# One ring for all first-layer weights, and preparation loads on GpSimd's queue

## The chip, the cores and the metric

The kernel runs on one core of a Trainium2 chip. Its time is the device time of the whole program in microseconds (us). Before the change three runs took 1879.51, 1882.88 and 1885.13 us, a median of 1882.88. TensorE (PE) does the matmuls, VectorE (DVE), ScalarE (ACT) and GpSimd (POOL) the work on elements. SyncE (SP), ACT and POOL also issue DMAs, each from a queue that it serves in order.

## The reference

```python
attn = softmax(q @ mean_pool8(k).T / 8) @ mean_pool8(v)     # 8 batches, 8 heads, 576 tokens, 64 wide
x    = attn as [4608, 512]
h    = x @ w_in                                             # [4608, 2048]
x2   = (s * relu(h)**2 + b) @ w_out                         # [4608, 512]
out  = (sigmoid(x2 @ w_gate) * (x2 @ w_val)) @ w_out2       # 1536 wide inside
```

Activations are float32. The weights of both layers come as 64-bit words and are turned into float32 on the chip. Every product of the two layers is made of three matmuls on a high and a low part of each operand.

## The kernel before, in words

The first layer works on blocks of 512 tokens: block 0 plainly, then four pairs of blocks by a scheme with fewer products (seven instead of eight; `LEFT`, L286), whose operands are sums and differences of the four quarters of the weights and of the activations. The second layer does the same with its weights. Attention runs beside the first layer in 18 units of 256 tokens, two units for each block, some time ahead of it.

A list of slots orders the first layer (L794). Slots 0 to 15 are block 0, then each pair `p` has 40 slots: slot 16 + 40 p + x with chunk x = 8 z + m, z the group of products and m one of eight row blocks. A slot makes up to one `h` step (`emit_h`, L259: 12 matmuls L269 to L271 with the tile `wi`, 512 KB) and one chunk of products (`mm_chunk`, L357: 6 or 12 matmuls L370 to L372 with the tile `wr`). In block 0 the products are `emit_x` (L419 to L421). From slot 16 on the order of PE and SP is the program's own (L835); the order of DVE, ACT and POOL is made by a planner that simulates the program.

**Weights.** For block 0, `load_wi` and `load_wo` load 64-bit words into a `raw` buffer (three of them, `rawp`), `split_wi` and `split_wo` convert them (`convert`, L78: one ACT and three DVE operations) and split them into a high and a low part (ACT, then POOL, L56 and L57). The results stay as tiles for PE and are stored to DRAM as `w1d` and `s1d` (list `later`, emptied by `store_later` at the start of the next slot, on SP up to slot 19 and on POOL after). All later blocks load these back on SP: `load_wi` (L137) three steps ahead into three buffers `wi`, `fetch_s` (L307, L312) into three buffers `wr`, each as soon as the buffer is free.

**Preparation.** In slots 16 to 31 `prep_s` makes the sums of quarters of the second weight, eight turns of two slots. Part 0 loads four tiles `s1d` into two `raw` buffers (L186, SP). Part 1 adds on DVE (L191), works on POOL (L179: four operations and the running sum `wsum`), splits (ACT, DVE) and hands four stores to POOL. `prep_bias` (L205) then sums `wsum` with the constant `b` on PE (`bps`, L212), at the start of slot 32, behind its `h` step. The bias is used by `put_x` (L344), which ends a group of products; for the first pair that is first at slot 33. From slot 33 on `prep_w2` (L228) prepares one second-layer block in eight slots (nine parts, 12 blocks; two parts a slot from x = 13 of the last pair): three loads of 512 KB into `raw` (L72, SP) and nine stores from POOL to `w7d` and `wo2d`. From step NS - 13 `gen_x` (L754) makes the first operands of the second layer.

Of the kernel before, what the change touches and what calls it, by code (L numbers as in the profile page):

```python
# [9 lines left out]
F32R = mybir.dt.float32r  # L10
I32 = mybir.dt.int32
# [8 lines left out]
def pooled_attention_two_ffn(ctx, tc, q, k, v, v_left, w_in, w_out, s_in, b_in, w_gate, w_val, w_out2, out):  # L20
# [46 lines left out]
    wo2d = [dram.tile([128, 2, 512], F32, name=f"wo2d{m}") for m in range(M2)]  # L67
    x2d = [dram.tile([128, KD, n], F32, name=f"x2d{j}") for j, (_, n) in enumerate(blocks)]

    def load64(src):  # L70
        raw = rawp.tile([128, 1024], I32, tag="raw", name="raw")
        nc.sync.dma_start(out=raw, in_=src.bitcast(I32))  # L72
        return raw

    def cv_tile():
# [21 lines left out]

    w1_stack = ExitStack()
    xp = w1_stack.enter_context(tc.tile_pool(name="xp", bufs=2))
    wi_p = w1_stack.enter_context(tc.tile_pool(name="wi_p", bufs=3))  # L100
    rawp = w1_stack.enter_context(tc.tile_pool(name="rawp", bufs=3))
    us_p = w1_stack.enter_context(tc.tile_pool(name="us_p", bufs=1))
    gs_p = w1_stack.enter_context(tc.tile_pool(name="gs_p", bufs=17))
    wr_p = w1_stack.enter_context(tc.tile_pool(name="wr_p", bufs=3))
    at_stack = ExitStack()
    at1 = at_stack.enter_context(tc.tile_pool(name="at1", bufs=1, side="right"))
    at2 = at_stack.enter_context(tc.tile_pool(name="at2", bufs=2, side="right"))
# [14 lines left out]
    bias = const.tile([128, KD], F32, name="bias")  # L122

    def wi_tile(i):
        t = wi_p.tile([128, 2, KD, 128], F32R, tag="wi", name="wi")
        wi[i] = t[:, 0], t[:, 1]
        return t.rearrange("p two k f -> p two (k f)")

# [45 lines left out]
    def prep_s(m, part):  # L174

        h0, h1 = slice(0, 256), slice(256, 512)

        def tt(o, x, y, op):
            nc.gpsimd.tensor_tensor(out=o, in0=x, in1=y, op=op)  # L179

        if part == 0:
            prep["s"] = []
            for xs in ((0, 7), (1, 3)):
                t = raw_tile().bitcast(F32).rearrange("p (two f) -> p two f", two=2)
                for h, x in zip((h0, h1), xs):
                    nc.sync.dma_start(out=t[:, :, h], in_=s1d[x][m])  # L186
                prep["s"].append(t)
        else:
            a, c = (t[:, 1] for t in prep["s"])
            for t in prep["s"]:  # L190
                nc.vector.tensor_tensor(out=t[:, 1], in0=t[:, 0], in1=t[:, 1], op=ALU.add)  # L191
            tt(c[:, h1], a[:, h1], c[:, h1], ALU.add)
            tt(a[:, h1], a[:, h0], a[:, h1], ALU.subtract)
            tt(a[:, h0], c[:, h1], a[:, h0], ALU.subtract)
            tt(c[:, h0], c[:, h0], a[:, h0], ALU.subtract)
            if m == 0:
                nc.gpsimd.tensor_copy(out=wsum, in_=c)
# [30 lines left out]
    def prep_w2(m, part):  # L228
        h0, h1 = slice(0, 256), slice(256, 512)
        if part == 0:  # L230
            prep["g"] = load64(w_gate[m])
        elif part == 1:
            prep["v"] = load64(w_val[m])
        elif part == 2:
            raw = prep["g"]
            prep["gt"] = convert(raw, cv_tile())
            store_split(w7d[m][:, :, 256:768], raw, prep["gt"])
        elif part == 3:
            prep["vt"] = convert(prep["v"], cv_tile())
            store_split(w7d[m][:, :, 0:256], raw_tile(), prep["vt"][:, h0])  # L240
        elif part == 4:
            gt, vt, c = prep["gt"], prep["vt"], cv_tile().bitcast(F32)
            for o, a, b_, op in ((c[:, h1], gt[:, h0], vt[:, h0], ALU.subtract), (vt[:, h0], vt[:, h0], vt[:, h1], ALU.add),
                                 (c[:, h0], vt[:, h0], gt[:, h0], ALU.subtract), (gt[:, h1], gt[:, h1], c[:, h0], ALU.subtract)):
                nc.gpsimd.tensor_tensor(out=o, in0=a, in1=b_, op=op)
            prep["c"] = c
        elif part == 5:
            store_split(w7d[m][:, :, 768:1280], prep["v"], prep["vt"])
        elif part == 6:
            store_split(w7d[m][:, :, 1280:1792], raw_tile(), prep["c"])  # L250
        elif part == 7:
            store_split(w7d[m][:, :, 1792:2048], raw_tile(), prep["gt"][:, h1])
            prep["o"] = load64(w_out2[m])
        else:
            store_split(wo2d[m], prep["o"], convert(prep["o"], cv_tile()))

# [95 lines left out]
    def keep(p, name, pair):  # L352
        acc[p, name] = [us_p.tile([128, 512], F32, tag=f"u{name}{d}", name="us") for d in range(2)]
        for o, a in zip(acc[p, name], pair):
            nc.scalar.activation(out=o, in_=a, func=ACTF.Copy)

    def mm_chunk(p, c):  # L357
        j, (z, m) = 1 + 2 * p, divmod(c, H1)
        if m == 0:
# [15 lines left out]
        if z == 0:  # L375
            keep(p, "p", acc[p, 0])
        elif z == 1:
            for d, a in enumerate(acc.pop((p, 0))):
                put_x(j, d, a)
        elif z == 2:  # L380
            keep(p, "v", acc[p, 2])
        elif z == 3:
            u, v = acc[p, "p"], acc[p, "v"]
            c12 = [cvp.tile([128, 512], F32, tag="cv", name="c12") for _ in range(2)]
            for d in range(2):
                add(u[d], acc[p, 3][d], u[d])
            for d in range(2):
                add(c12[d], acc[p, 2][d], u[d])
            for d in range(2):
                add(v[d], v[d], u[d])  # L390
                put_x(j + 1, d, c12[d])
            del acc[p, 3], acc[p, 2]
        else:
            u, v = acc.pop((p, "p")), acc.pop((p, "v"))
            for d in range(2):
                add(v[d], acc[p, 5][d], v[d])
                add(u[d], acc[p, 5][d], u[d])
            for d in range(2):
# [283 lines left out]
    def turns(u, t):  # L682
        turn(u, t, 0)
        turn(u, t, 1)

    with tc.manual_schedule():
        load_kv(0, "k")
        load_q(0, 2)
# [10 lines left out]
        nc.vector.tensor_tensor(out=mask[:, 2:3], in0=mask[:, 0:1], in1=mask[:, 1:2], op=ALU.subtract)  # L699
        pool_k(0, 0, nc.vector)  # L700
        pool_k(0, 1, nc.vector)
        load_wi(0)
# [4 lines left out]
        load_wi(1)  # L707
        probs(0, 0)
        probs(0, 1)
        norm(0, 0, True)  # L710
# [9 lines left out]
        place_left(0)  # L720
        turns(0, 1)
        norm(1, 0, True)
        split_wi(0)
# [6 lines left out]
        split_wi(1)  # L730
        turns(1, 1)
    if True:
        values(1, 0)
        values(1, 1)
        load_wi(2)
        load_q(2)
        load_q(3)
        NS = len(steps)
        LAG = 2


        pairs = [(1024 * p, 512) for p in range(NB // 2)]
# [46 lines left out]
            sub(b21, b21, b22)  # L789
            put(3, b21)  # L790

        chunks = [(None, i) for i in range(M1)] + [(p, x) for p in range(NB1) for x in range(5 * H1)]  # L794
        NSLOT = len(chunks)
        hidden, used, made, done = {}, [], {}, {}
        for slot, (p, x) in enumerate(chunks):
            if p is None:
                hidden[slot] = x
                ready, turn_ = slot + 5, slot + 6  # L800
            else:
                if x < 4 * H1:
                    hidden[slot if p == 0 or x > 1 else slot - H1] = M1 * (1 + 2 * p) + x
                ready, turn_ = slot, slot + LAG
                if p == 0 and x < H1:
                    ready, turn_ = M1 + 5 + x // 2, M1 + 6 + x // 2
            made.setdefault(ready, []).append((p, x))
            done.setdefault(turn_, []).append((p, x))
            if p is None or x >= 3 * H1 or x % 2:
                used.append((turn_, p, x))  # L810
        asked = M1

        def mm(slot):
            for p, x in done.get(slot, []):
                if p is None:
# [15 lines left out]
        for slot, (p, x) in enumerate(chunks):  # L831
            i = hidden.get(slot)
            swap = p is not None and x == 4 * H1 + 1
            if slot == M1:
                pe_order.enter_context(tc.manual_schedule(engines={mybir.EngineType.PE, mybir.EngineType.SP}))  # L835
            store_later(slot < M1 + 4)
            for fn, args in events.pop(2 * slot, []):
                fn(*args)
            if i is not None:
                load_wi(i + 3)  # L840
                if not swap:
                    emit_h(i)
            for m, r in parts.get(slot, []):
                prep_w2(m, r)
            if M1 <= slot < 2 * M1:
                prep_s(*divmod(slot - M1, 2))
            if slot == 2 * M1:
                prep_bias()
            if slot < M1:
                split_wi(i + 2)  # L850
            if 4 <= slot < M1 + 4:
                split_wo(slot - 4)
            if 2 <= slot < M1 + 2:
                load_wo(slot - 2)
            late = []
            for p1, x1 in made.get(slot, []):
                if p1 is None:
# [12 lines left out]
                    prep_chunk(p1, x1, 1)  # L870
            if swap and i is not None:
                emit_h(i)
            while asked < len(used) and used[asked - 3][0] <= slot:
                _, p1, x1 = used[asked]
                fetch_s(p1, x1 - (x1 < 3 * H1))
                asked += 1
            if p is not None and 4 * H1 - 2 <= x < 5 * H1 - 2:
                reload(p, x - 4 * H1 + 2)
            if i == NS - M1:
# [185 lines left out]
```

## Time and profile before

| | |
|---|---|
| median of three runs | 1882.88 us |
| profiled execution | 1877.16 us, span 1875.3 us |
| PE busy | 1732.0 us (92%), mean granted clock 0.964 |
| DVE, ACT, POOL busy | 1073.2, 751.1, 473.6 us |
| DMA | 464.94 MB, mean 248 GB/s |

The first layer ends at about 1050 us; from there PE is never idle for long until the end. "Idle before" and "waits" name the time in which an engine had nothing running and what it waited for; an engine named SPq, POOLq or ACTq is its DMA queue. A wait of several causes is put down to the one that came last. PEclk is the clock that TensorE was granted, as a part of 2.4 GHz. A row of a timeline gives start and duration in us.

### The profile page before, as it was taken

The page shows a single profiled execution, that of the slowest core. Times are in us where ns is not written, and L with a number is a line of the kernel's source. Part 1 is how long each engine was busy: PE and PEld are TensorE (multiplying, and loading weights), DVE is VectorE, ACT ScalarE, POOL GpSimd, SP SyncE. Part 2 cuts the span into 40 slices and gives each one's busy share as a digit, 9 for nine tenths or more (in the row PEclk, how much of TensorE's full clock was granted, in tenths as well). Part 3 has the DMA queues.
Part 4 walks back from the last instruction along what each step waited for, and adds up shares of the span by engine and source line. Part 5 has one row for each costly group of instructions (what it writes and reads, how often), then busy time and mean ns, then how long its engine had stood idle before and what let it go on. Part 6 is the DMA issues. An engine that isn't in the chain of part 4 may idle for free.

```text
span 1875.3 us, 22252 instructions
## 1 busy us (share of the span) xinstructions
PE 1732.0 (92%) x7880; PEld 1428.1 (76%) x7880; DVE 1073.2 (57%) x1653; ACT 751.1 (40%) x1331; POOL 473.6 (25%) x558
## 2 busy tenths in 40 slices
PE   5899776998999899999849999999999999999999
PEld 4677665876888688877737788888888888888887
DVE  7788554776775868576546544454545544544211
ACT  3676443645664456456534322222222222222111
POOL 4644655435730655005430000100010001000100
PEclk7899987999999999999979999999999999999999
DMA  6878987887976888677856755665576558555675
GB/s 240 284 240 287 337 284 251 279 312 250 372 271 223 288 311 308 226 274 264 320 203 208 251 187 200 252 225 202 201 252 225 184 184 292 185 190 211 224 239 181
DMA packets 153917, 464.94 MB, mean 248 GB/s; under 512 B 16336, under 2 KB 34256, under 8 KB 153808
## 3 DMA queue, kind: packets, MB, share of 16 engines
q1 hardware_dynamic: 127344, 388.55, 59.1%
q0 software_dynamic: 16672, 57.16, 8.5%
q10 hardware_dynamic: 9792, 17.83, 2.5%
q8 instruction: 63, 1.03, 0.2%
q14 instruction: 46, 0.38, 0.1%
HBM read 379.59 MB, written 83.89 MB: 247 GB/s over the span
## 4 chain that ended last, share of the span: by engine, by line
PE 71%; DMA 12%; DVE 11%; POOL 2%; ACT 2%; issue 2%; SPq 1%; ACTq 0%; POOLq 0%; DVEq 0%
PE acc L967 5%; PE pc L912 5%; PE acc L969 5%; PE acc L968 5%; PE pc L913 5%; PE pc L911 5%; PE hps L269 4%; PE hps L271 4%; PE hps L270 4%; PE pb L911 4%; PE pb L912 4%; PE pb L913 4%; DMA raw<-in 4%; PE acc L370 3%; PE acc L371 3%; PE acc L372 3%
## 5 line engine op out<-in xcount | busy, mean ns | idle before, releaser
L269 PE MATMUL hps<-xl,wi 128*128 128x512 f32 (+1 forms) x584 | 237.9, 407 | 51.8 <-DMA wi<-w1d 44.8
L917 DVE TENSOR_TENSOR wk<-pc,wk 128x512 f32<-128x512 f32 x192 | 132.4, 690 | 240.4 <-PE pc L913 240.4
L271 PE MATMUL hps<-xh,wi 128*128 128x512 f32 (+1 forms) x584 | 232.3, 398 | 1.1 <-POOL wi L57 1.1
L270 PE MATMUL hps<-xh,wi 128*128 128x512 f32 (+1 forms) x584 | 232.1, 397 | 0.0
L370 PE MATMUL acc<-gl,wr 128*128 128x512 f32 x448 | 183.0, 409 | 17.7 <-DMA wr<-s1d 10.4
L977 POOL DMA_DIRECT2D out<-eo x32 | 17.4, 544 | 705.1 <-ACT eo L975 702.3
L371 PE MATMUL acc<-gh,wr 128*128 128x512 f32 x448 | 177.9, 397 | 0.0
L372 PE MATMUL acc<-gh,wr 128*128 128x512 f32 x448 | 177.5, 396 | 0.0
L928 ACT ACTIVATE g<-pb 128x512 f32<-128x512 f32 x60 | 35.9, 599 | 346.7 <-PE pb L913 346.7
L269 PEld LDWEIGHTS hps<-xl,wi 128*128 128x128 f32 x584 | 114.2, 196 | 78.4 <-issue 38.5
L57 DVE TENSOR_TENSOR gl<-gs,gh 128x512 fp32r<-128x512 f32 x176 | 149.5, 862 | 37.1 <-ACT gh L56 34.3
L911 PE MATMUL pc<-xo,w 128*128 128x512 f32 x432 | 168.1, 389 | 0.0
L912 PE MATMUL pc<-xo,w 128*128 128x512 f32 x432 | 168.1, 389 | 0.0
L913 PE MATMUL pc<-xo,w 128*128 128x512 f32 x432 | 168.0, 389 | 0.0
L57 POOL TENSOR_TENSOR raw<-cv,raw 128x512 fp32r<-128x512 f32 (+1 forms) x72 | 89.8, 1253 | 295.9 <-ACT raw L56 149.5
L56 ACT ACTIVATE gh<-gs 128x512 fp32r<-128x512 f32 x176 | 107.3, 627 | 114.0 <-DVE gs L296 98.7
L56 ACT ACTIVATE gh<-g 128x512 fp32r<-128x512 f32 x124 | 77.8, 628 | 154.2 <-DVE g L929 141.7
L911 PE MATMUL pb<-xo,w 128*128 128x512 f32 x336 | 131.4, 391 | 2.2 <-DMA w<-w7d 2.2
L271 PEld LDWEIGHTS hps<-xh,wi 128*128 128x128 f32 x584 | 113.6, 195 | 25.8 <-POOL wi L57 1.6
L57 DVE TENSOR_TENSOR gl<-g,gh 128x512 fp32r<-128x512 f32 x124 | 106.5, 859 | 44.7 <-ACT gh L56 40.1
L912 PE MATMUL pb<-xo,w 128*128 128x512 f32 x336 | 131.4, 391 | 0.0
L913 PE MATMUL pb<-xo,w 128*128 128x512 f32 x336 | 131.3, 391 | 0.0
(142 smaller groups left out, 3739.5 us busy)
## 6 DMA issues: line engine op xcount, KB each, us to landing
w<-w7d SPq DMA_DIRECT2D x48, 1792.0 KB, 7.7
wi<-w1d SPq DMA_DIRECT2D x128, 512.0 KB, 5.1
wr<-s1d SPq DMA_DIRECT2D x224, 256.0 KB, 4.9
wo<-wo2d SPq DMA_DIRECT2D x108, 512.0 KB, 7.9
raw<-in SPq DMA_DIRECT2D x68, 512.0 KB, 5.8
w7d<-raw POOLq DMA_DIRECT2D x36, 512.0 KB, 5.5
w<-w7d SPq DMA_DIRECT2D x12, 1280.0 KB, 6.8
kv<-in SPq DMA_DIRECT2D x24, 512.0 KB, 6.5
```

The lines of the kernel that those rows point to most:

```text
L56: nc.scalar.activation(out=hi, in_=src, func=ACTF.Copy)
L57: eng.tensor_tensor(out=lo, in0=src, in1=hi.bitcast(F32), op=ALU.subtract)
L269: nc.tensor.matmul(out=ps[:, f], lhsT=hi[:, kk], rhs=c[:, kk, f], start=kk == 0, stop=False)
L270: nc.tensor.matmul(out=ps[:, f], lhsT=hi[:, kk], rhs=a[:, kk, f], start=False, stop=False)
L271: nc.tensor.matmul(out=ps[:, f], lhsT=lo[:, kk], rhs=a[:, kk, f], start=False, stop=kk == KD - 1)
L370: nc.tensor.matmul(out=a, lhsT=w[:, 0, f], rhs=gl, start=begin, stop=False, skip_group_check=True)
L371: nc.tensor.matmul(out=a, lhsT=w[:, 0, f], rhs=gh, start=False, stop=False, skip_group_check=True)
L372: nc.tensor.matmul(out=a, lhsT=w[:, 1, f], rhs=gh, start=False, stop=end, skip_group_check=True)
L911: nc.tensor.matmul(out=ps, lhsT=w[:, 0, x, kk], rhs=r[:, 1, kk, :n], start=first and kk == 0, stop=False, skip_group_check=True)
L912: nc.tensor.matmul(out=ps, lhsT=w[:, 0, x, kk], rhs=r[:, 0, kk, :n], start=False, stop=False, skip_group_check=True)
L913: nc.tensor.matmul(out=ps, lhsT=w[:, 1, x, kk], rhs=r[:, 0, kk, :n], start=False, stop=kk == 1, skip_group_check=True)
L917: nc.vector.tensor_tensor(out=o, in0=ps, in1=b_, op=ALU.add)
```

## The change

- The pool `wi_p` (three buffers) is gone and `wr_p` has six (`RING`). `wi_tile` takes its tile from it, so `wi` and `wr` tiles share one ring.
- Before the slots a list `used` is made: every first-layer weight tile of the ring with the slot in which PE uses it and the slot after which it is free, sorted by use. `ask(slot)`, at the end of a slot, asks for tiles in this order while the tile six places back is free by this slot and the use is at most three slots off. For block 0 asking means `split_wi` or `split_wo`, and the next 64-bit load (`ask_raw`, in the order of use) goes out behind it. The separate calls of `load_wi`, `split_wi`, `split_wo`, `load_wo` and `fetch_s` in the loop are gone.
- The loads of `prep_s` (32 of 256 KB) and of `prep_w2` (36 of 512 KB) are issued from GpSimd (`nc.gpsimd`) instead of SP.
- `store_later` puts stores on SP in slots below 12 instead of below 20.
- `prep_bias` moves from slot 32 to slot 38, and the first pair's first two `put_x` (`put_c11`) from the end of chunk x = 15 to the same place.

```diff
-    def load64(src):
+    def load64(src, eng=None):
         raw = rawp.tile([128, 1024], I32, tag="raw", name="raw")
-        nc.sync.dma_start(out=raw, in_=src.bitcast(I32))
+        (eng or nc.sync).dma_start(out=raw, in_=src.bitcast(I32))
...
-    wi_p = w1_stack.enter_context(tc.tile_pool(name="wi_p", bufs=3))
...
-    wr_p = w1_stack.enter_context(tc.tile_pool(name="wr_p", bufs=3))
+    RING = 6
+    wr_p = w1_stack.enter_context(tc.tile_pool(name="wr_p", bufs=RING))
...
-        t = wi_p.tile([128, 2, KD, 128], F32R, tag="wi", name="wi")
+        t = wr_tile().rearrange("p (two k f) -> p two k f", two=2, k=KD)
...
-                    nc.sync.dma_start(out=t[:, :, h], in_=s1d[x][m])
+                    nc.gpsimd.dma_start(out=t[:, :, h], in_=s1d[x][m])
...
-            prep["g"] = load64(w_gate[m])
+            prep["g"] = load64(w_gate[m], nc.gpsimd)
-            prep["v"] = load64(w_val[m])
+            prep["v"] = load64(w_val[m], nc.gpsimd)
...
-            prep["o"] = load64(w_out2[m])
+            prep["o"] = load64(w_out2[m], nc.gpsimd)
...
+    def put_c11(p):
+        for d, a in enumerate(acc.pop((p, 0))):
+            put_x(1 + 2 * p, d, a)
...
         elif z == 1:
-            for d, a in enumerate(acc.pop((p, 0))):
-                put_x(j, d, a)
+            if p:
+                put_c11(p)
...
-            if p is None or x >= 3 * H1 or x % 2:
-                used.append((turn_, p, x))
+        if p is None or x >= 3 * H1:
+            used.append((turn_, 1, turn_, p, x))
+        elif x % 2 == 0:
+            used.append((turn_, 1, turn_ + (p > 0 or x >= H1), p, x))
+    used += [(slot, 0, slot, "h", i) for slot, i in hidden.items()]
+    used.sort(key=lambda u: u[:2])
...
+    def ask(slot):
+        nonlocal asked
+        while asked < len(used) and (asked < RING or used[asked - RING][2] <= slot) and used[asked][0] <= slot + 3:
+            _, _, _, k, x = used[asked]
+            asked += 1
+            if k == "h" and x < M1:
+                split_wi(x)
+                ask_raw()
+            elif k == "h":
+                load_wi(x)
+            elif k is None:
+                split_wo(x)
+                ask_raw()
+            else:
+                fetch_s(k, x)
...
-            store_later(slot < M1 + 4)
+            store_later(slot < M1 - 4)
...
-                load_wi(i + 3)
...
-            if slot == 2 * M1:
+            if slot == 2 * M1 + 6:
                 prep_bias()
+                put_c11(0)
-            if slot < M1:
-                split_wi(i + 2)
-            if 4 <= slot < M1 + 4:
-                split_wo(slot - 4)
-            if 2 <= slot < M1 + 2:
-                load_wo(slot - 2)
...
-            while asked < len(used) and used[asked - 3][0] <= slot:
-                _, p1, x1 = used[asked]
-                fetch_s(p1, x1 - (x1 < 3 * H1))
-                asked += 1
+            ask(slot)
```

## Rows read from the trace of the kernel before

**Rows 1.** Busy time by stretch: stretch, length, engines' busy us (instructions), PEclk, DMA share, GB/s

```profile
160.00:336.00 176.00, 139.79 (x661) 115.42 (x660) 99.69 (x159) 76.46 (x141) 102.87 (x120) 0.89 0.84 288
200.00:337.00 137.00, 100.79 (x464) 82.24 (x463) 73.38 (x120) 56.06 (x103) 80.66 (x98) 0.86 0.83 283
917.00:985.00 68.00, 35.04 (x137) 27.30 (x136) 34.18 (x45) 29.63 (x53) 28.95 (x37) 0.78 0.64 226
```

**Rows 2.** Waits of PE, 200 to 345 us: line, releaser, us in total, times, longest

```profile
PE bps L212 <- DVE wsum L207: 13.5, 1, 13.5
PE hps L269 <- DMA wi<-w1d: 12.5, 4, 5.9
PE acc L370 <- DMA wr<-s1d: 7.1, 2, 6.8
```

**Rows 3.** Waits of PE, 900 to 1053 us

```profile
PE hps L269 <- DMA wi<-w1d: 32.3, 3, 25.8
```

**Rows 4.** Waits of SP's DMA queue, 150 to 310 us

```profile
SPq L186 <- DMA s1d<-raw: 54.1, 6, 11.3
```

**Rows 5.** Timeline of SP's DMA queue: start, us, line, issue

```profile
211.92 12.20 SPq L186 DMA_DIRECT2D raw<-s1d  x4
...
225.34 0.84 SPq L307 DMA_DIRECT2D wr<-s1d  x2
```

**Rows 6.** Waits of SP's DMA queue, 900 to 985 us

```profile
SPq L72 <- DMA w7d<-raw: 49.1, 4, 32.2
```

**Rows 7.** Timeline of SP's DMA queue in the second stretch

```profile
974.87 0.40 SPq L137 DMA_DIRECT2D wi<-w1d  x1
```

**Rows 8.** Timeline of PE: start, us, line, matmul, shape, count, idle before and its releaser

```profile
286.66 0.63 PE L270 MATMUL hps<-xh,wi 128*128 128x512 f32 x1
287.08 0.63 PE L271 MATMUL hps<-xh,wi 128*128 128x512 f32 x1
...
302.54 2.05 PE L212 MATMUL bps<-cv,wsum 128*128 128x128 f32 x8 [13.54 <-DVE wsum L207]
...
336.26 0.39 PE L271 MATMUL hps<-xh,wi 128*128 128x512 f32 x1
336.50 0.60 PE L607 MATMUL tm<-ident,pm 128*128 128x128 f32 x4
```

**Rows 9.** Timeline of POOL, first and last two turns of prep_s, and one later row

```profile
174.09 3.92 POOL L179 TENSOR_TENSOR raw<-raw 128x256 f32<-128x256 f32 x4 [4.96 <-DVE raw L191]
...
282.65 3.15 POOL L179 TENSOR_TENSOR raw<-raw 128x256 f32<-128x256 f32 x4 [2.64 <-DVE raw L191]
...
287.61 2.82 POOL L152 DMA_DIRECT2D s1d<-raw  x4
296.36 3.13 POOL L179 TENSOR_TENSOR raw<-raw 128x256 f32<-128x256 f32 x4 [5.93 <-DVE raw L191]
299.57 1.77 POOL L179 TENSOR_TENSOR wsum<-wsum,raw 128x512 f32<-128x512 f32 x1
...
927.11 2.19 POOL L57 TENSOR_TENSOR raw<-cv,raw 128x512 fp32r<-128x512 f32 x2
```

**Rows 10.** Groups by line, POOL, 150 to 310 us: busy us, mean ns, idle before

```profile
L152 POOL DMA_DIRECT2D s1d<-raw x28 | 19.8, 806 | 1.9 <-DVE raw L57 1.9
```

**Rows 11.** DMA issues, 160 to 336 us: count, KB each, us to landing

```profile
raw<-s1d SPq DMA_DIRECT2D x32, 256.0 KB, 4.7
s1d<-raw POOLq DMA_DIRECT2D x28, 256.0 KB, 3.3
```

**Rows 12.** Timeline of DVE, 924 to 932 us

```profile
924.55 5.30 DVE L57 TENSOR_TENSOR gl<-gs,gh 128x512 fp32r<-128x512 f32 x1 [0.70 <-ACT gh L56]
...
931.16 0.69 DVE L57 TENSOR_TENSOR gl<-gs,gh 128x512 fp32r<-128x512 f32 x1 [0.70 <-ACT gh L56]
```

**Rows 13.** Part 2 of the page: GB/s in 40 slices of the span

```profile
GB/s 240 284 240 287 337 284 251 279 312 250 372 271 223 288 311 308 226 274 264 320 203 208 251 187 200 252 225 202 201 252 225 184 184 292 185 190 211 224 239 181
```

**Rows 14.** Waits of PE, 0 to 1000 us

```profile
PE tm L607 <- POOL pm L582: 10.5, 6, 3.9
```

More of the change, by code (lines that the diff above doesn't have):

```diff
@@ L684, in turns, with ask_raw, ask_one @@
         turn(u, t, 1)
+    NS = len(steps)
+    LAG = 2
+    chunks = [(None, i) for i in range(M1)] + [(p, x) for p in range(NB1) for x in range(5 * H1)]
+    NSLOT = len(chunks)
+    hidden, used, made, done = {}, [], {}, {}
+    for slot, (p, x) in enumerate(chunks):
+        if p is None:
+            hidden[slot] = x
+            ready, turn_ = slot + 5, slot + 6
+        else:
+            if x < 4 * H1:
+                hidden[slot if p == 0 or x > 1 else slot - H1] = M1 * (1 + 2 * p) + x
+            ready, turn_ = slot, slot + LAG
+            if p == 0 and x < H1:
+                ready, turn_ = M1 + 5 + x // 2, M1 + 6 + x // 2
+        made.setdefault(ready, []).append((p, x))
+        done.setdefault(turn_, []).append((p, x))
+        if p is None or x >= 3 * H1:
[4 more added lines that the diff above has]
+    used.sort(key=lambda u: u[:2])
+    halves = [(k, x) for _, _, _, k, x in used if k is None or k == "h" and x < M1]
+    asked = raws_asked = 0
+    def ask_raw():
+        nonlocal raws_asked
+        if raws_asked < len(halves):
+            k, x = halves[raws_asked]
+            raws_asked += 1
+            if k == "h":
+                load_wi(x)
+            else:
+                load_wo(x)
+    def ask_one():
+        nonlocal asked
+        split_wi(used[asked][4])
+        asked += 1
+    def ask(slot):
+        nonlocal asked
+        while asked < len(used) and (asked < RING or used[asked - RING][2] <= slot) and used[asked][0] <= slot + 3:
+            _, _, _, k, x = used[asked]
+            asked += 1
+            if k == "h" and x < M1:
+                split_wi(x)
+                ask_raw()
+            elif k == "h":
+                load_wi(x)
+            elif k is None:
+                split_wo(x)
+                ask_raw()
+            else:
+                fetch_s(k, x)
     with tc.manual_schedule():
@@ L701, in pooled_attention_two_ffn @@
         pool_k(0, 1, nc.vector)
-        load_wi(0)
+        ask_raw()
         load_kv(0, "l")
@@ L706, in pooled_attention_two_ffn @@
         nc.sync.dma_start(out=b_sb, in_=b_in.unsqueeze(0).to_broadcast([128, 1]))
-        load_wi(1)
+        ask_raw()
         probs(0, 0)
@@ L722, in pooled_attention_two_ffn @@
         norm(1, 0, True)
-        split_wi(0)
+        ask_one()
         values(0, 0)
@@ L729, in pooled_attention_two_ffn @@
         left(1, 1)
-        split_wi(1)
+        ask_one()
         turns(1, 1)
@@ L734, in pooled_attention_two_ffn @@
         values(1, 1)
[L735 removed]
+        ask_raw()
         load_q(2)
         load_q(3)
[L738 to L739 removed]
         pairs = [(1024 * p, 512) for p in range(NB // 2)]
@@ L790, in gen_x @@
             put(3, b21)
[L794 to L808, printed above, removed]
-            if p is None or x >= 3 * H1 or x % 2:
-                used.append((turn_, p, x))
-        asked = M1
         def mm(slot):
@@ L835, in pooled_attention_two_ffn @@
                 pe_order.enter_context(tc.manual_schedule(engines={mybir.EngineType.PE, mybir.EngineType.SP}))
-            store_later(slot < M1 + 4)
+            store_later(slot < M1 - 4)
             for fn, args in events.pop(2 * slot, []):
                 fn(*args)
-            if i is not None:
-                load_wi(i + 3)
-                if not swap:
-                    emit_h(i)
+            if i is not None and not swap:
+                emit_h(i)
             for m, r in parts.get(slot, []):
```

## The prediction, made before the changed kernel ran

> **What bounds the kernel now.** I read three views in this order: the busy time by stretch, the waits of PE, and the issue queue of SP at the places where PE waits. PE is the bound wherever nothing stops it, so I looked for the stretches in which it stops. There are two. From 200 to 337 us PE is busy 100.8 of 137 us at a mean granted clock of 0.86, and from 917 to 985 us it is busy 35.0 of 68 at 0.78 [rows 1].
>
> Stretch A is slots 22 to 38. PE's waits there are 13.5 us for the sum `wsum` in front of the bias product, 12.5 us for the tile `wi`, and 7.1 us for the tile `wr` [rows 2]: 33.1 us. Stretch B lies in the last pair of first-layer blocks (slots 152 to 160): 32.3 us, all for `wi`, 25.8 of them at once [rows 3].
>
> In neither stretch is the transfer slow; it is issued late. SP's queue is served in order, and in A the loads of `prep_s` (L186) stand in it for 54.1 us, waiting until an earlier store has left the `raw` buffer they want [rows 4]. One of them holds the queue from 211.92 for 12.2 us [rows 5], and the `wr` load that PE then waits for stands behind it. In B it is the second-layer preparation load (L72), which waits 49.1 us for `w7d` stores [rows 6]; the load of `wi` goes out right after it, at 974.87 [rows 7].
>
> A stop costs a second time. After a long one the granted clock has dropped from the 2.4 to the 1.2 GHz level, and matmuls start 0.42 us apart instead of 0.24 [rows 8]. About a dozen run so before the clock is back, 12 x 0.19 = 2.3 us. A has four such stops (the 13.5 us, one of 6.8, one of 5.9 and one a little shorter), so 9.2 us; B has two, so 4.6.
>
> **The change part by part.** *SP's queue freed in A.* The 32 loads of `prep_s` leave SP, and its weight loads now wait only for a ring tile. Six tiles in order of use reach three slots ahead, as the two pools of three did, so I give the ring itself nothing: the landing it must cover is the same, and the price if that cover went is one landing a slot. What goes at most is 33.1 + 9.2 = 42.3 us.
>
> *What is late next in A.* The bias product still needs all eight turns of `prep_s`. It is now asked for at slot 38. Before, PE went from its end (302.54 + 2.05) to the same place in slot 38 (336.50) in 31.9 us [rows 8]. With every stall of A but the bias wait gone, PE would have been at slot 32's product at 289.0 - 19.6 (the two DMA waits) - 6.9 (three restarts) = 262.5, and so at slot 38 at 294. Is `wsum` there by then?
>
> The chain of `prep_s` is serial through three `raw` buffers: store, load into the same buffer, add, four GpSimd operations and a sum, split, store. Its first turn began on POOL at 174.09, the last two at 282.65 and 296.36 [rows 9]. So the fastest turn takes 13.7 us, the mean 122.3 / 7 = 17.5. On POOL a DMA issue costs 0.81 us [rows 10]. Four loads are added a turn; those into the free buffer are hidden in the landing of the stores (3.3 us), the other two are not [rows 11]: 2 x 0.81 = 1.6 us, and with a little for a later landing I add 1.9 us a turn (what SP's own issues took there I don't subtract). At 15.6 us a turn the last one starts at 283 and `wsum` is ready 5 us later, at 288; at 19.4 us, at 310 and 315. These are the two ends. A second count decides between them: POOL is busy 80.7 us of A [rows 1], 24 loads of the six turns in it add 24 x 0.81 = 19, together 100 us; with no idle at all that is 300, and with one microsecond lost a turn 306. I take 306. The bias product (2.05 us) then ends at 308 instead of work at that place starting at 336.5: 28.5 us, less 2.3 for the clock after a wait of 13 us: **26 us in A**. The ends give 42 (ready before PE) and 17.
>
> Moving `put_c11` to slot 38 holds two accumulators of PSUM six slots longer. Slots 34 to 41 use the other two, so it costs nothing unless the product slips past slot 42.
>
> *SP's queue freed in B.* At most 32.3 + 4.6 = 36.9 us. The preparation loads now wait on POOL, where nothing of PE's stands behind them so late: no attention is left after slot 150. What can be late next is DVE: it is busy 34.2 us in this stretch [rows 1], about as long as the PE work in it, because conversions of second-layer weights run there at two parts a slot and the first second-stage operands are generated. DVE and ACT work in order, so an operand of PE's can stand behind a conversion whose load has not landed. The ends are all of the 36.9 and less than half (14, if the chain of `raw` buffers still sets the pace through DVE). I take a quarter lost: **27 us in B**.
>
> *Other moves.* The 36 second-layer loads add 36 x 0.81 = 29 us to POOL over 700 us and take as much waiting off SP: nothing, since POOL has idle time beside them outside A; if that cover went it would be the 29 us. Some 16 stores move from SP to POOL in slots 12 to 19, 13 us of POOL before A begins, and the splits of the first block are asked for one slot earlier, on engines that the planner orders. I see nothing that excludes a loss or a gain there: between -6 and +6 us, half the 13 either way; I take 0.
>
> *Sum.* 26 + 27 = 53 us. The profiled execution took 1877.16 us around a span of 1875.3; less 53 that is 1824. The median of the runs, 1882.88, lies 5.7 above the profiled execution, so I predict **1830 us**.
>
> *A rule against it.* One DVE subtraction that elsewhere takes 0.69 us took 5.30 at 924.55 [rows 12], while POOL ran one operation after another; two of them are the 2.19 us at 927.11 [rows 9]. So the two engines do hold each other off here, and more work on POOL makes such runs longer. The Trainium skill, page "SBUF — State Buffer", section "SBUF: two separate sides", says that DVE and GpSimd share one pair of ports under an exclusive lock for a whole instruction, and that descriptors of a DMA issued from GpSimd cannot be written while DVE holds it; the traces agree on the lock, and of starved descriptors they show nothing, since POOL's stores land in 3.3 us and SP's loads in 4.7. By that rule the time would be the first rival's below, by these rows the forecast's.
>
> **The rivals.** *POOL and DVE hold each other off.* If every load on POOL also waits out one DVE operation of 0.69 us [rows 12], a turn takes 19.4 + 4 x 0.69 = 22.2 us, the last one starts at 329, `wsum` comes at 334 and A gives nothing; with 25 us of B the time is 1858. For it: POOL would be nearly full in A. Against: the store landings just named. Chance 0.17. The lock that the Trainium skill states on its page "SBUF — State Buffer" is this rival's ground too.
>
> *Nothing is late next.* If the turns run at 15.6 us and DVE's order keeps conversions behind operands, 42 + 37 = 79 us go: 1804. For it: the last turns already ran at 13.7. Against: POOL has 100 us of work for 94 us. The transfers also speak against it: A and the slots before it move 288 GB/s over 176 us [rows 1], 50.7 MB; by 294 instead of 336 that would be 378 GB/s, above the best slice of the page, 372 [rows 13]. For the forecast's 306 it is 347. Chance 0.15.
>
> *It goes slower.* The wait is not removed, it moves to POOL's queue, and behind it there stand the probabilities `pm`, on which PE's transposes wait already (10.5 us in six places) [rows 14]. If the planner puts a waiting load in front of most of them, SP's 54.1 and 49.1 us of waiting reach PE again by that way, and the 68 issues of 0.81 us, 55 us, come on top of them on the same queue. With a third of these 55 on PE's path the time is 1882.9 + 18 = about 1900; it decides once more than 53 us of waits at `pm` and at the operands are new. Against: POOL is idle 56 of A's 137 us, and POOL's order is the planner's, not written out. Chance 0.08.
>
> *It does not do what it says.* SP may stop again, now at loads of `wr` that read what `prep_s` stored late (third group of products, slots 34 to 41), with `wi` behind them. If all of A's gain goes so and B's is eaten by conversions, the time stays within 0.3%. Chance 0.06.
>
> **How the numbers follow.** The forecast has 0.54, with its own range of 1812 to 1848 (17 to 42 in A and 14 to 37 in B, not both ends at once). Faster by over 0.3% are the forecast, the first rival and the second: 0.54 + 0.17 + 0.15 = 0.86. Within 0.3%, about 6 us and all that can be told from no change here: 0.06. Slower: 0.08. For 8 in 10 I leave out the slower end with no change (0.14) and some of the second rival's far side: 1802 to 1863.
>
> **What would show it.** In the trace after, SP's list of waits should hold no L186 and no L72, and POOL's should hold loads of `raw`. PE's wait for `wi` should fall from 44.8 us over the first stage to a few. The bias product should start near 306, with a wait of up to 13 us for `wsum`; a start before 295 is the second rival, after 325 the first. In B the 25.8 us stop should be gone, with small waits for `gl` in its place. New waits at `pm` of over 4 us each would show the slower case. The forecast is wrong if the turns of `prep_s` come further apart than 20 us, or if B still has a stop of over 10 us.

## The result, and the profile after

The changed kernel takes 1854.86 us (median of four runs, 1852.52 to 1861.10) against 1881.2 us before: a ratio of 0.9863, 95% interval 0.9831 to 0.9894. That is 26 us, half of the 53 forecast; it lies in the range of 1802 to 1863, but outside the forecast's own 1812 to 1848. The profiled execution has a span of 1851.4 us against 1875.3.

Where the 23.9 us come from is seen by setting the same matmul of both timelines side by side. Each mark is the start of the first L370 matmul (L374 after) of that slot:

| mark | before | after | after is ahead by |
|---|---|---|---|
| slot 34, third group of the first pair | 315.96 | 276.43 | 39.5 |
| slot 42, behind the bias product of both | 356.15 | 372.88 | -16.7 |
| slot 154 | 916.88 | 922.13 | -5.2 |
| slot 162 | 988.52 | 955.57 | 33.0 |
| first matmul of the second layer | 1053.10 | 1030.82 | 22.3 |
| end of the span | 1875.3 | 1851.4 | 23.9 |

So the first stretch was won and then lost with interest, and the second was won in full. Two smaller pieces moved beside them: 11.5 us won between slots 42 and 154, which the prediction had at nothing, and 10.7 lost at the end of the first layer. These marks come from one execution of each kernel, so a difference of a few us in them is not proof by itself.

The windows of after, with the columns of [rows 1]:

```profile
200.00:337.00 137.00, 96.28 (x500) 80.69 (x498) 79.63 (x124) 57.71 (x104) 83.94 (x103) 0.88 0.70 239
917.00:985.00 68.00, 67.51 (x298) 55.59 (x297) 51.84 (x68) 42.93 (x77) 31.85 (x39) 1.00 0.93 311
```

In the second stretch PE now runs through at full clock where it was busy 35 of 68 us [rows 1]. In the first it does 500 matmuls instead of 464, and yet it stands still at the end of it. PE's waits from 160 to 1050 us say where (line, releaser, us in total, times, longest); SP's longest of 150 to 345 us and POOL's two longest of 160 to 352 us name the two other places:

```profile
PE bps L212 <- POOL cv L245: 50.8, 1, 50.8
PE acc L374 <- DVE c L350: 10.0, 4, 5.0
```

```profile
SPq L307 <- DMA s1d<-raw: 67.8, 6, 17.7
```

```profile
POOL raw L186 <- DMA s1d<-raw: 14.5, 5, 4.8
POOL s1d L152 <- DVE raw L57: 13.8, 7, 4.0
```

No wait for a `wi` tile from DRAM is left where there were 44.8 us [rows 2, 3]. All of the first stretch's loss is one wait, in front of the bias product. The releaser in its row is not to be believed: the product does not read what L245 writes. What it needed last is found in the order of ACT, below.

### The profile page after: what moved, and what is told of

Same layout as the page of the kernel before. It is cut to its first block, busy times and chain, and to the rows that moved or that the text cites. A ratio compares the mean times of both kernels' runs of the same rounds, so it can differ in the third digit from the quotient of the medians.

```text
span 1851.4 us, 22232 instructions
## 1 busy us (share of the span) xinstructions
PE 1717.3 (93%) x7880; PEld 1420.4 (77%) x7880; DVE 1081.0 (58%) x1653; ACT 751.2 (41%) x1331; POOL 536.0 (29%) x646
## 3 DMA queue, kind: packets, MB, share of 16 engines
q0 software_dynamic: 26144, 90.19, 13.7%
q8 instruction: 63, 1.03, 0.2%
## 4 chain that ended last, share of the span: by engine, by line
PE 59%; DMA 8%; DVE 7%; POOL 3%; issue 2%; ACT 1%; SPq 0%; ACTq 0%; DVEq 0%; POOLq 0%
PE pc L945 5%; PE pc L943 5%; PE pc L944 5%; PE acc L999 5%; PE acc L1001 5%; PE acc L1000 5%; PE pb L945 4%; PE pb L943 4%; PE pb L944 4%; PE hps L269 2%; PE hps L271 2%; PE hps L270 2%; PE acc L374 2%; PE acc L375 2%; PE acc L376 2%; DVE gl L57 2%
## 5 line engine op out<-in xcount | busy, mean ns | idle before, releaser
L269 PE MATMUL hps<-xl,wr 128*128 128x512 f32 (+1 forms) x584 | 233.0, 399 | 6.1 <-DVE xl L57 3.9
L271 PE MATMUL hps<-xh,wr 128*128 128x512 f32 (+1 forms) x584 | 229.4, 393 | 0.9 <-POOL wr L57 0.9
L270 PE MATMUL hps<-xh,wr 128*128 128x512 f32 (+1 forms) x584 | 229.2, 393 | 0.0
L374 PE MATMUL acc<-gl,wr 128*128 128x512 f32 x448 | 181.3, 405 | 18.6 <-DVE c L350 10.0
L269 PEld LDWEIGHTS hps<-xl,wr 128*128 128x128 f32 x584 | 112.1, 192 | 28.2 <-DVE xl L57 4.1
L271 PEld LDWEIGHTS hps<-xh,wr 128*128 128x128 f32 x584 | 111.9, 192 | 24.8 <-POOL wr L57 1.2
L270 PEld LDWEIGHTS hps<-xh,wr 128*128 128x128 f32 x584 | 112.1, 192 | 21.4
```

Source lines behind the costliest of these rows:

```text
L269: nc.tensor.matmul(out=ps[:, f], lhsT=hi[:, kk], rhs=c[:, kk, f], start=kk == 0, stop=False)
L270: nc.tensor.matmul(out=ps[:, f], lhsT=hi[:, kk], rhs=a[:, kk, f], start=False, stop=False)
L271: nc.tensor.matmul(out=ps[:, f], lhsT=lo[:, kk], rhs=a[:, kk, f], start=False, stop=kk == KD - 1)
L374: nc.tensor.matmul(out=a, lhsT=w[:, 0, f], rhs=gl, start=begin, stop=False, skip_group_check=True)
```

## Why the sum was late: one turn, row by row

The timeline of POOL after, one turn of `prep_s` (start, us, line, operation, count, idle before and its releaser):

```profile
262.64 2.86 POOL L152 DMA_DIRECT2D s1d<-raw  x4 [0.85 <-DVE raw L57]
...
265.27 1.56 POOL L586 TENSOR_TENSOR pm<-e,sm 128x512 f32<-128x512 f32 x1
271.43 1.49 POOL L186 DMA_DIRECT2D raw<-s1d  x2 [4.59 <-DMA s1d<-raw]
274.21 1.45 POOL L186 DMA_DIRECT2D raw<-s1d  x2 [1.29 <-issue]
276.69 3.87 POOL L179 TENSOR_TENSOR raw<-raw 128x256 f32<-128x256 f32 x4 [1.03 <-DVE raw L191]
```

From the first store (262.64) to the next turn's first operation (276.69) it takes 14.1 us. In the last turn of before it took 296.36 - 287.61 = 8.75 [rows 9], and there the load went out from SP:

```profile
291.27 1.18 SPq L186 DMA_DIRECT2D raw<-s1d  x2
```

So the 5.3 us more lie between store and load: 8.8 us now (262.64 to 271.43), 3.7 then (287.61 to 291.27). From load to operation it is 5.3 and 5.1. In both kernels the load waits until the store has left the buffer. What grew is the time until the stores land, and POOL stands for the last 4.59 us of it and does nothing else meanwhile. The pair at 274.21 is already a load of the turn after next. It stands in POOL's order in front of the work, but POOL waits for DVE behind it (1.03), so it costs nothing here.

The DMA issues of after, 160 to 336 us (count, KB each, us to landing):

```profile
s1d<-raw POOLq DMA_DIRECT2D x28, 256.0 KB, 5.2
raw<-s1d POOLq DMA_DIRECT2D x28, 256.0 KB, 4.2
```

The stores took 3.3 us before [rows 11]. Within this kernel the stores of 262 to 274 us, and those of 303 to 310 us when PE stands, took:

```profile
s1d<-raw POOLq DMA_DIRECT2D x4, 256.0 KB, 8.2
```

```profile
s1d<-raw POOLq DMA_DIRECT2D x4, 256.0 KB, 3.0
```

The DMA engines are busy 0.91 of the first of these stretches and 0.55 of the second. That the weight loads, which SP now sends without a stop, make the stores late fits this but is not shown: over 160 to 336 us less is moved than before (256 GB/s against 288 [rows 1]). The issues are not slow: 1.45 us a pair of loads, 0.73 each, less than the 0.81 of the stores [rows 10], and four stores take 2.86 us to issue, as before (2.82 [rows 9]).

Not every turn is like this one. The first operations of the eight turns are 39.3, 25.1, 23.3, 20.7, 19.7, 16.9 and 16.4 us apart, where they were 19.1, 20.4, 14.2, 21.8, 17.1, 16.0 and 13.7. Half of the 39 us that the chain loses lie in the first distance, and the last two turns, in which PE stands, are nearly as before. In the first distance the load of the second turn has landed at 196.4 (issued at 192.61, 3.8 us to landing), but DVE adds only at 206.75, in its order behind work that waited for ACT:

```profile
198.84 0.90 DVE L57 TENSOR_TENSOR gl<-gs,gh 128x512 fp32r<-128x512 f32 x1 [5.31 <-ACT gh L56]
...
206.75 0.69 DVE L191 TENSOR_TENSOR raw<-raw 128x512 f32<-128x512 f32 x1
```

That is 10.3 us from landing to addition. Where the loads are on SP (before, and two of the kernels below) it is 0.1 to 0.2 us; in two others with the loads on GpSimd it is 6.7 and 11.3. So DVE's order, the planner's own, is a second part of the delay.

From the first to the eighth turn it is 168.27 to 329.60 us, 23.0 us a turn against 17.5 [rows 9]; the last addition to `wsum` ends at 334.8 and DVE's sum of its halves at 337.3. PE stands from 299.0. It starts at 349.73, and the missing 12.4 us are in the order of ACT:

```profile
346.70 0.68 ACT L85 ACTIVATE cv<-raw 128x512 f32<-128x512 f32 x1 [11.80 <-DMA raw<-in]
...
349.24 0.39 ACT L209 ACTIVATE cv<-ident,b_sb 128x128 f32<-128x128 f32 x1
```

L209 writes the constant operand of the bias product. It needs no late data, but stands behind the conversion L85, and that waits for a second-layer load that POOL, being late, issued only at 340.20.

## The experiments

All ratios are against runs of the kernel before on the same chip. These were taken in four sets, with medians of before of 1881.2 us (the changed kernel), 1877.55 (the experiments on second-layer loads alone, on `prep_s` back on SP, on a fourth buffer on GpSimd and on the early constant), 1880.59 (ring alone, five ring tiles, the two with four buffers and `prep_s` on SP) and 1886.03 (the last four). So kernels of different sets are compared by ratio, 0.01 being about 19 us. Times inside a kernel are from its one profiled execution. "Turn" below is the mean distance between the ends of the second and the eighth addition to `wsum`: 16.8 us before (200.6 to 301.3) and 20.5 in the changed kernel (212.1 to 334.8).

**Only the second-layer loads on GpSimd.**

```diff
-            prep["g"] = load64(w_gate[m])
+            prep["g"] = load64(w_gate[m], nc.gpsimd)
...
-            prep["o"] = load64(w_out2[m])
+            prep["o"] = load64(w_out2[m], nc.gpsimd)
```

> The kernel before with one edit: the 36 second-layer preparation loads are issued from GpSimd instead of SP. Theory (the gain after slot 152 comes from taking these loads out of SP's queue, the ring has no part in it): the 25.8 us stop of PE at the wi load near 957 us goes, the stretch from 917 to 985 us gives 32 to 38 us, the first stretch stays as before (bias product near 302 us); about 1846 us. Rival (the ring's order or depth gives it): PE stops there as before, about 1881 us.

1859.55 us, ratio 0.990 (0.987 to 0.993). The stop is gone: from slot 154 to slot 162 it takes 33.1 us instead of 71.6, the same 38 us that the whole change gives there. So that gain is these 36 loads' alone. Its total is less, by 4 us at the start, 7 between slots 42 and 154 and 10 at the end of the first layer.

**The ring alone**, with everything else of the change undone.

```diff
-    wi_p = w1_stack.enter_context(tc.tile_pool(name="wi_p", bufs=3))
...
-    wr_p = w1_stack.enter_context(tc.tile_pool(name="wr_p", bufs=3))
+    RING = 6
+    wr_p = w1_stack.enter_context(tc.tile_pool(name="wr_p", bufs=RING))
...
+            ask(slot)
```

> The changed kernel with all of the change undone except the ring and its order of asking: prep_s and second-layer loads on SP, stores on SP to slot 19, bias product and put_c11 at their old places. Theory (the ring has a share of its own that the prediction set at nothing: from the bias product to slot 152 the changed kernel takes 549 us where the kernel with only the second-layer loads moved takes 568): 8 to 18 us less than before, about 1862; the stop at wi near 957 us stays in some length. Rival (the ring alone gives nothing, what was gained there is the late bias's own backlog catching up): 1874 to 1882.

1865.77 us, ratio 0.9917 (0.9898 to 0.9936): some 15 us. The stop at `wi` in the second stretch stays, 27.3 us long. The profiled execution gains 6 us between slots 42 and 154, 3 in the second stretch and 3 at the end of the layer. The ring, with its order of asking, has a share of its own.

**The loads of `prep_s` back on SP**, the rest of the change kept.

```diff
-                    nc.gpsimd.dma_start(out=t[:, :, h], in_=s1d[x][m])
+                    nc.sync.dma_start(out=t[:, :, h], in_=s1d[x][m])
```

> The changed kernel with the 32 loads of prep_s back on SP. Theory (the turns of prep_s became slow because on POOL each turn's loads stand behind the stores of the turn before and their landing, and POOL cannot compute in between): turns fall from 23 us back to about 17.5, the sum wsum is ready near 305 us instead of 337 and the 50.8 us wait of PE at the bias product falls to 20 or less; SP's queue stops again in slots 20 to 31 and PE loses some 15 to 25 us there; in sum about 1835 to 1850 us. Rival (the turns are slow because the faster PE starves them, by transfers or by DVE): turns stay over 20 us, and with SP's stops added the time is 1865 or more.

1838.6 us, ratio 0.9783 (0.976 to 0.9807): 15 to 16 us faster than the changed kernel. The turn is 16.8 us again, the last addition ends at 303.5, and PE does not wait at the bias product, which starts at 330.85. The price is SP's: its waits for the `raw` buffer, 150 to 310 us, and PE's waits, 200 to 345 us.

```profile
SPq L186 <- DMA s1d<-raw: 71.2, 7, 16.6
```

```profile
PE hps L269 <- DMA wr<-w1d: 26.9, 6, 6.1
```

So one wait has two places where it can stand. On POOL the weights flow, the turns are longer and PE waits 50.8 us for the product; on SP the wait holds the weights and costs PE 26.9. The stores land in 3.4 us here (160 to 336 us), but PE is stopped again, so this run alone does not tell whether GpSimd's queue or the faster PE made the turns long.

**A fourth `raw` buffer**, the loads staying on GpSimd; a ring tile gives the room.

```diff
-    rawp = w1_stack.enter_context(tc.tile_pool(name="rawp", bufs=3))
+    rawp = w1_stack.enter_context(tc.tile_pool(name="rawp", bufs=4))
...
-    RING = 6
+    RING = 5
```

> The changed kernel with four raw buffers instead of three, and five ring tiles instead of six to make room. Theory (the wait for stores to leave the raw buffer, on POOL, makes the turn): with two buffers for each of two turns the loads need no landing of the turn before, turns fall below 17 us, wsum is ready before 300 us, PE's wait of 50.8 us at the bias product goes nearly all; about 1805 to 1815 us. Rival (POOL's own work, 84 us of 137 there, or DVE, sets the turn): turns stay over 20 us and the time within 8 us of 1855.

1826.55 us, ratio 0.9707 (0.9674 to 0.974), less than expected. The turn falls to 15.7 us, but the second addition ends only at 223.4, and the eighth at 317.3, so PE still waits 20.6 us at the product. The first 100 us of the stretch, changed kernel first and this one second:

```profile
200.00:300.00 100.00, 96.28 (x500) 80.69 (x498) 62.88 (x101) 49.58 (x91) 59.40 (x73) 1.00 0.78 270
```

```profile
200.00:300.00 100.00, 99.45 (x514) 83.95 (x513) 72.15 (x104) 50.62 (x93) 74.65 (x94) 0.99 0.90 317
```

With three buffers POOL is busy only 59 us of 100. It was not full, it was waiting. With four it does 94 instructions instead of 73 in the same time. Part of that is the order and not the buffer: the next kernel, with three buffers and five ring tiles, does 88 there and is busy 70.7 us. The stores land no sooner (5.5 us, 160 to 336 us), and yet the turn is shorter: with the fourth buffer the loads need not wait for them. Why the second addition is so late is not shown.

**Five ring tiles**, nothing else, as the control for it.

```diff
-    RING = 6
+    RING = 5
```

> The changed kernel with five ring tiles instead of six, nothing else: the control for the kernel with four raw buffers. Theory (a tile more or less in the ring hardly matters while SP is not stopped): within 5 us of the changed kernel, about 1856, turns of prep_s at 23 us as there. Rival (the fifth against the sixth tile shifted the planner's order, and that made the gain of the kernel with four raw buffers): near 1827.

1853.23 us, ratio 0.9851 (0.9834 to 0.9869), and PE waits 51.3 us at the product. The sixth tile does not matter; the fourth `raw` buffer made the gain. The product starts at 343.36 here and at 321.39 with the fourth buffer, 22 us earlier; 10.8 of these are the sum's, the rest ACT's order, which holds the product 12.9 us behind the sum here and 1.7 there.

**The constant operand made in slot 2.**

```diff
-        bb = cv_tile().bitcast(F32)[:, 0:128]
-        nc.scalar.activation(out=bb, in_=ident, func=ACTF.Identity, scale=0.0, bias=b_sb)
+        bb = bb_sb
...
+            if slot == 2:
+                nc.scalar.activation(out=bb_sb, in_=ident, func=ACTF.Identity, scale=0.0, bias=b_sb)
```

> The changed kernel with the constant operand of the bias product made in slot 2, into a tile of its own, instead of in slot 38. Theory (of the 50.8 us wait the last 12.4 are ACT's: the constant stands in ACT's queue behind a conversion whose load POOL issues late, while wsum is summed by 337.3 us): the bias product starts some 12 us earlier, near 338 us, and the time falls by 8 to 12 us to about 1844. Rival (PE is held there by the stores and loads of s1d in any case, or the same wait comes back two slots later at the wr tiles): the bias product starts earlier but the time stays within 4 us of 1855.

1855.92 us, ratio 0.9881 (0.985 to 0.9912): no change. The product does start 10.7 us earlier, at 339.03, released by DVE's sum of `wsum`. At slot 42 PE is still 11 us ahead, at slot 154 only 0.6. That ACT's order held the product is shown, but not where the time was given back: new waits of PE for DVE between those slots sum to it only in part, and the planner's order differs throughout. This stays open.

**Four `raw` buffers and the loads on SP.**

```diff
-    rawp = w1_stack.enter_context(tc.tile_pool(name="rawp", bufs=3))
+    rawp = w1_stack.enter_context(tc.tile_pool(name="rawp", bufs=4))
...
-    RING = 6
+    RING = 5
...
-                    nc.gpsimd.dma_start(out=t[:, :, h], in_=s1d[x][m])
+                    nc.sync.dma_start(out=t[:, :, h], in_=s1d[x][m])
```

> The changed kernel with the loads of prep_s back on SP, four raw buffers and five ring tiles. Theory (the wait for the raw buffer is what hurts, on whichever queue it stands): with the fourth buffer SP hardly waits at these loads, so its stops of 4 to 6 us in slots 22 to 31 (27 us in sum with three buffers) go, turns stay below 17 us and PE does not wait at the bias product; 1838.6 - 20 to 27 = about 1815. Rival (SP's order of issue itself makes those stops, not the wait for a buffer): stops of PE at its ring tiles stay, 1830 or more.

1801.81 us, ratio 0.9589 (0.9552 to 0.9625): 79 us faster than before, 51 to 53 faster than the changed kernel. The turn is 13.4 us, the last addition ends at 281.4, 24 us before PE asks at 305.8. SP's waits at these loads, 150 to 310 us, PE's waits for ring tiles, 200 to 345 us, and the windows of the first 100 us:

```profile
SPq L186 <- DMA s1d<-raw: 28.2, 10, 7.7
```

```profile
PE hps L269 <- DMA wr<-w1d: 3.5, 3, 2.2
```

```profile
200.00:300.00 100.00, 93.38 (x473) 77.09 (x473) 75.10 (x113) 53.27 (x99) 77.39 (x94) 0.98 0.96 351
```

SP still waits 28 us there, but in pieces of 7.7 us at most, and PE's waits for ring tiles are nearly gone. PE is busy 93 us of these 100 and the DMA engines 0.96 of the time at 351 GB/s. Both are near full; which of them bounds the stretch now is not shown.

**The same with the constant made early.** On top of the last kernel:

```diff
-        bb = cv_tile().bitcast(F32)[:, 0:128]
-        nc.scalar.activation(out=bb, in_=ident, func=ACTF.Identity, scale=0.0, bias=b_sb)
+        bb = bb_sb
...
+            if slot == 2:
+                nc.scalar.activation(out=bb_sb, in_=ident, func=ACTF.Identity, scale=0.0, bias=b_sb)
```

> As the kernel with the loads on SP and four raw buffers, and the constant operand of the bias product made in slot 2. Theory: where wsum is ready before PE asks, ACT's queue is the only thing left that can hold the product, by a few us; 0 to 5 us less than without it. Rival (the planner's other order decides): a difference of either sign of more than 5 us.

1801.89 us, ratio 0.9575 (0.9558 to 0.9593): the same. Nothing waits at the product any more, so nothing is gained.

**Four `raw` buffers, with the loads of `prep_s` and of the second layer on SP.**

```diff
-            prep["g"] = load64(w_gate[m], nc.gpsimd)
+            prep["g"] = load64(w_gate[m])
...
-            prep["o"] = load64(w_out2[m], nc.gpsimd)
+            prep["o"] = load64(w_out2[m])
```

> The kernel with four raw buffers and prep_s on SP (1801.8 us), and now the second-layer loads on SP too: nothing is issued from GpSimd that was not before. Theory (a load that waits for its buffer stops the queue it stands in; four buffers take away the wait of prep_s but not that of the last second-layer blocks, which run at two parts a slot beside the first second-stage operands): the stop of PE at wi after slot 152 comes back in part, 10 to 25 us, about 1815 to 1825. Rival (with four buffers no load waits long, and the move to GpSimd was never needed): within 4 us of 1802.

1829.4 us, ratio 0.9708 (0.9656 to 0.9761): the move of these 36 loads is worth 22 us by the ratios (28 by the medians) even with four buffers. From 850 to 1053 us PE waits for ring tiles again:

```profile
PE hps L269 <- DMA wr<-w1d: 23.2, 4, 16.6
```

**The fastest kernel (four `raw` buffers, `prep_s` loads on SP) with the bias product at slot 32.**

```diff
-            if p:
-                put_c11(p)
+            put_c11(p)
...
-            if slot == 2 * M1 + 6:
+            if slot == 2 * M1:
                 prep_bias()
-                put_c11(0)
```

> The kernel with four raw buffers and prep_s on SP, with the bias product and put_c11 back at slots 32 and 33. Theory: its wsum is ready at 281 us and PE comes to slot 32 about 30 us before it comes to slot 38 (306 us), so it waits some 5 to 8 us and loses 2 more by the clock: 1805 to 1812; the six slots are worth that much, no more. Rival (PE has other slack there): within 3 us of 1802.

1810.45 us, ratio 0.9613 (0.9567 to 0.9659): 8.6 us more by the medians, 4.5 by the ratios, whose intervals overlap: not clear of noise. PE waits 6.1 us at the product and starts it at 279.58; at slot 42 the profiled execution is 8 us behind.

**The fastest kernel with five `raw` buffers and four ring tiles.**

```diff
-    rawp = w1_stack.enter_context(tc.tile_pool(name="rawp", bufs=4))
+    rawp = w1_stack.enter_context(tc.tile_pool(name="rawp", bufs=5))
...
-    RING = 5
+    RING = 4
```

> The kernel with prep_s on SP, with five raw buffers and four ring tiles. Theory: the fifth buffer takes the rest of SP's waits at these loads (28 us with four), but four ring tiles are two slots ahead at most where a slot takes two, less than the 6 us a load needs with its wait in the queue; stops of PE at ring tiles come back, 1805 to 1820. Rival (the buffers of raw are all that matters): 1797 or less.

1813.16 us, ratio 0.9615 (0.9569 to 0.9661). That is 11 us more by the medians, 5 by the ratios, not clear of noise. PE waits 24.6 us for ring tiles over the first layer, in 13 places, where five tiles left 4.6. The fifth buffer does take SP's waits at these loads (3.1 us instead of 28.2), but the sum gains nothing: the last addition ends at 281.0. As both were changed at once, their prices are not parted.

**The fastest kernel with the stores of slots 12 to 19 back on SP.**

```diff
-            store_later(slot < M1 - 4)
+            store_later(slot < M1 + 4)
```

> The kernel with four raw buffers and prep_s on SP, with the stores of slots 12 to 19 back on SP. Theory (16 stores of 0.8 us on POOL before the turns of prep_s are off PE's path, as the prediction took them): within 5 us of 1802. Rival (they delay the first turns of prep_s on POOL): wsum is ready earlier than 281 us and the time falls by more than 5 us.

1805.63 us, ratio 0.9587 (0.9536 to 0.9639): no difference. The second addition is done 8.5 us earlier (192.6), the first 8 us later and the last 1.4 later (282.8). The first distance between turns is 19.8 us instead of 29.1. It is 19 to 20 in every kernel that has these stores on SP, and 25 to 39 in all others; the stores of the first turn of `prep_s` are among them. Here the sum has 24 us to spare, so this run does not tell what the move of the stores cost the changed kernel, where PE waits for the sum.

## Why the prediction was half right

*What bounds the kernel* held. Both stretches were stops of SP's queue, and taking the loads out of it took the stops away. At slot 34 the changed kernel is 39.5 us ahead, close to the 42.3 us ceiling for A; the 13.5 us for the sum are among them, but they were only put off to slot 38.

*B* held, with its loss elsewhere. It won 38.2 us between slots 154 and 162, all that was there, where I took 27 by giving a quarter to DVE. PE waits for DVE later: from 988 us to the end of the layer it waits 12.9 us for the sums of L350; the kernel before has no such wait there. That and the clock behind these stops are taken as the cause of the 10.7 us lost at the end; 38.2 - 10.7 is 27.5.

*A* failed, and the step is one term of the sum: "I add 1.9 us a turn". By the count that the prediction used, it is 23.0 us a turn against 17.5, so 5.6 were added. That is beyond its end of 19.4 and beyond the 20 us that it had itself named as the sign of a wrong forecast. I had priced the issues on POOL, at 1.6 us, and left 0.3 for a later landing of the stores. In the turn read above the later landing alone is 5 us; and DVE's order in the first turn, 10 us, had no term at all. The second count, POOL's busy time of 100 us, chose 306 us for the product because it treated POOL as full; the changed kernel's POOL is busy 59 of 100. Of the 50.8 us of waiting, 38 are the late sum (299.0 to 337.3) and 12.4 ACT's order, which the prediction did not see. So instead of 26 won, A has 16.7 lost at slot 42.

*The time lies in the range by luck in part.* A came out 43 us worse than forecast. The 11.5 us between slots 42 and 154, which the sum did not have, made up for some of it; without them the time would be about 1866 us, above the range.

*The first rival* gave A nothing, 22.2 us a turn, `wsum` at 334 and 1858 us in all. Its numbers came close, but A lost 16.7 us, and its mechanism is not what the rows show. It let DVE hold up each load's issue, and the issues take 0.73 us each. The prediction's other sign against it, stores that land in 3.3 us, is gone: they land in 5.2. The lock itself shows in the first turn, where DVE's split at 184.13 takes 4.72 us instead of 0.69, so a small share of it is not excluded. The *slower* rival put the moved wait in front of `pm`: PE's waits at `pm` went from 10.5 [rows 14] to 9.2 us over the first layer. The rival by which SP stops again, at loads of `wr` that read what `prep_s` stored late, did come about: these are SP's 67.8 us above. PE's own stop at the product covers them.

*The ring at nothing* was wrong by some 15 us. Depth was not the gain, since five tiles do as well as six. That leaves tiles shared in order of use, or the places at which they are asked for; the runs do not part these two. Nor is it sure that the ring made the 11.5 us between slots 42 and 154: alone it gains 6 there, and the other kernels with the ring gain between 1 and 16.

*The six slots* are worth 4 to 9 us with four buffers, not clear of noise. With three buffers they were too few: the product would have had to move 50 us, and the `wr` loads of the next group wait for the same turns anyway (SP's 67.8 us above).

## What to carry to other kernels

A load that waits for its buffer stops whatever queue it is put in: first ask how many buffers the loop needs so that a load never waits for a store to land, and only then where to issue it. When you price a chain of store and load through one buffer, do not take the landing times of the kernel before: here, with SP's queue freed, the stores landed in 5 to 8 us instead of 3.3, for a cause that the runs do not isolate. The Trainium skill, page "DMA: Bandwidth & Descriptors", section "Issuing engines are not separate DMA queues", says that starting DMAs from several engines saves only the time of the sequencer. For `prep_s` this case agrees that nothing is gained: with four buffers it takes 1801.8 us from SP and 1826.6 from GpSimd. For the second-layer loads the move was worth 22 us or more, because it took a wait, not an issue, out of SP's queue.

## What the runs showed that I had not expected

POOL's 256 KB stores land in 3.3 us before [rows 11], 5.2 in the changed kernel and 6.6 in the fastest (160 to 336 us), where the DMA engines are busiest (0.92 of that time). Their share alone does not set it: it is 0.84 before and 0.74 in the changed kernel. In the fastest kernel the chain of `prep_s` is the fastest of these three although its stores land last: with a fourth buffer the next load need not wait for them. And 351 GB/s over 100 us, with the DMA engines 0.96 busy, is above what I had taken the forecast to need (347).
